# A hand-written instruction order for windowed attention with a gated convolution block: score folding, masking, biasing, convolution taps and reciprocals split into pieces of their own, and a new order of the period

## The chip, the cores and the metric

The kernel runs on one core of one Trainium2 chip. The metric is the device time of one execution in microseconds (us), measured over several executions; the profile is one further execution, recorded by the hardware profiler. A core has five instruction streams that matter here: TensorE (PE in the profile, with its weight loads shown apart as PEld), VectorE (DVE), ScalarE (ACT), GpSimd (POOL) and SyncE (SP, which here only issues DMAs). Each stream is executed in the order in which it was written; streams wait for each other on semaphores.

## The reference

Attention over 8 batches, 8 heads, 576 positions and head size 64, in a causal window of 128 with a linear distance bias, followed by a block that projects 512 to 1024 channels, applies a three-tap convolution along the sequence, gates with a sigmoid and projects back. All of it is in float32.

```python
scores = scale * np.matmul(q, k.transpose(0, 1, 3, 2))
bias = slopes[:, None, None] * (-np.abs(rel).astype(np.float32))[None, :, :]
mask = (rel >= 0) & (rel < window)
scores = np.where(mask, scores + bias[None], -1000000000.0)
scores = scores - np.max(scores, axis=-1, keepdims=True)
attn = np.exp(scores)
attn = attn / (np.sum(attn, axis=-1, keepdims=True) + 1e-09)
x = np.matmul(attn, v)
...
h = np.maximum(x @ w_in, 0.0)
for k in range(K):
    conv_out += conv_w[k][None, None, :] * hp[:, k:k + S, :]
gate = 1.0 / (1.0 + np.exp(-conv_out))
return (h * gate @ w_out)
```

## The kernel before

The 8 x 576 = 4608 tokens are cut into 36 tiles of 128, numbered t = 0 to 35, without regard to the batches' borders. Each tile's eight heads are worked in two groups of four, u = 0 and 1. Two tiles make a chunk of 256 columns for the convolution block; a chunk has four steps s, each over two blocks of 128 hidden channels, ff = 0 and 1. So a tile goes with two steps. The weights stay resident, each split into a high and a low part, and a product with full precision is three matmuls.

The order of all work is written out by hand. Three strings, OPENING, PERIOD and TAIL (lines 584 to 619), list pieces by short names; `emit` (line 570) calls the function behind each name, and under `tc.manual_schedule` every engine executes its instructions in just that order. OPENING holds tiles 0 to 5 and the splitting of the weights, PERIOD is emitted once for each of the 30 tiles 6 to 35, with the names' first number relative to the tile or to its first step, and TAIL finishes the last steps. In a name such as `T0.1` the first number is the tile (or step) and the second the group u (or the block ff); -1 is the tile or step before.

The pieces of a tile, with their engine, are:

- `S` (line 326, TensorE): the scores of one group, as many small matmuls, into two PSUM tiles `sc`, one for each half a = 0 and 1 of the group (two heads each). A query's window touches three blocks of 64 keys, of which two fill the 128 regular columns and the third 64 extra ones.
- `MA` (function `merge`, line 336, VectorE): for one half, a predicated copy that folds the extra columns into the regular ones (line 347); in tiles at a batch border (t mod 9 is 0, 4 or 5) one more predicated copy that writes a large negative value (line 355); then scale and bias, from PSUM into the SBUF tile `e` (line 358).
- `RM` (line 362, VectorE): the row extremum of the group's four heads. `X` (line 367, ScalarE): the exponentials with their sums, two heads to a piece.
- `N` (function `normal`, lines 378 and 379, VectorE): adds 1e-9 to the sums and takes the reciprocal. `M` (line 384, GpSimd): multiplies `e` by it.
- `T` (line 390, TensorE): four transposes of `e` into a PSUM tile `pa`. `RL` (line 395, ScalarE): copies that to SBUF as `rl`. `SEL` (lines 401 and 404, GpSimd): splits `rl` into the part for this tile's values and the part for the tile before.
- `AV` (line 420, TensorE): the product with the values for the tile before, group 0 first and then group 1. `XH` (line 431, ScalarE) and `XL` (line 435, VectorE) split the result into high and low part, and `XF` (lines 449 and 451, VectorE) copies one border column between neighbouring chunks. The first step of a chunk needs the border column of the tile behind it, so in every second period the period's first `UH` needs the `XF` of the same period.
- `QV` (line 244, VectorE): transposes the next tile's queries and keys. `LB`, `LV` (SyncE): loads.

The pieces of a step are:

- `UH` (line 464, TensorE): 12 matmuls into a PSUM tile `p`. `HH` (line 472, ScalarE): the rectifier. `Z` (line 478, ScalarE): the middle tap, into the PSUM tile `zp`, of which there is one buffer.
- `CV` (function `conv`, line 491, VectorE): the two outer taps, one after the other, both added in place into `zp`; where a batch border lies in the chunk, each tap is cut in two.
- `TH` (line 498, ScalarE): the tanh form of the gate. `GT` (line 502, VectorE): the gated product. `GH` (line 509, ScalarE) and `GL` (line 514, GpSimd): its high and low part.
- `D` (line 528, TensorE): 12 matmuls of the down projection. `OB` (line 538, ScalarE, and a store by SyncE): the result, every second period.

The PSUM tiles `sc`, `av`, `p` and `pa` share five buffers, and a new one takes a buffer that an earlier one has left.

Of the kernel before, what the change touches and what calls it, by code (L numbers as in the profile page):

```python
# [21 lines left out]
def tile_alibi_window_attention_conv_glu(  # L22
# [227 lines left out]
    raws, vraw, pts, sms, es, pas, rls, avs = {}, {}, {}, {}, {}, {}, {}, {}  # L250
# [82 lines left out]
        sms[t, u] = pss  # L333


    def merge(t, u, a):
# [10 lines left out]
        nc.vector.copy_predicated(  # L347
            out=s_all.rearrange("p g (c w) -> p g c w", w=QW),
            mask=m_same.rearrange("p (c w) -> p c w", w=QW).unsqueeze(1).to_broadcast([P, NG, NQ, QW]),
            data=extra,  # L350
        )
        negb = neg.unsqueeze(2).to_broadcast(shp)
        masks = [m for m, on in ((m_prev, first == 0), (m_half, first + P > S), (m_after, 0 < first < P)) if on]
        for mask in masks:
            nc.vector.copy_predicated(out=s_all, mask=mask.unsqueeze(1).to_broadcast(shp), data=negb)  # L355
# [2 lines left out]
        nc.vector.scalar_tensor_tensor(out=heads, in0=s_all, scalar=-0.125, in1=b, op0=ALU.mult, op1=ALU.add)  # L358

# [4 lines left out]
    def exps(t, u, heads=range(HU)):  # L364
        e, st, pss = sms[t, u]
        for j in heads:
            nc.scalar.activation(  # L367
                out=e[:, j, :],
                in_=e[:, j, :],
                func=AF.Exp,  # L370
                bias=st[:, 0, j : j + 1],
                scale=-1.0,
                accum_out=st[:, 1, j : j + 1],
            )

    def normal(t, u):
        e, st, pss = sms.pop((t, u))
        nc.vector.tensor_scalar(out=st[:, 2, :], in0=st[:, 1, :], scalar1=1e-9, scalar2=None, op0=ALU.add)
        nc.vector.reciprocal(out=st[:, 2, :], in_=st[:, 2, :])  # L379
        es[t, u] = e, st  # L380

# [97 lines left out]
            out=zps[s][:, ff, :], in_=hhs[s][:, ff, 1 : 1 + CW], func=AF.Copy, scale=cw[:, 1, f : f + 1]  # L479
        )  # L480

    def conv(s, ff):
# [4 lines left out]
        for kk, cuts in ((0, starts), (2, [x - 1 for x in starts])):
            a = 0
            for cut in [x for x in cuts if 0 <= x < CW] + [CW]:
                if cut > a:  # L490
                    nc.vector.scalar_tensor_tensor(  # L491
                        out=z[:, ff, a:cut], in0=hh[:, ff, a + kk : cut + kk], scalar=cw[:, kk, f : f + 1],
                        in1=z[:, ff, a:cut], op0=ALU.mult, op1=ALU.add,
                    )
                a = cut + 1

    def tanh(s):
        nc.scalar.activation(out=zps[s], in_=zps[s], func=AF.Tanh)  # L498
# [85 lines left out]
    OPENING = """
    LD0 F0 LD1 LV0 F1 F2 F3 F4 LD2 LV1 F5 Q0 CL0 QO0 S0.0 S0.1 RS0 Q1 MA0.0.0 MA0.1.0 MA0.1.1 MA0.0.1
    QO1 RM0.1 V0 F6 X0.1.1 S1.0 CL1 CL2 MA1.0.0 RM0.0 S1.1 X0.1.0 X0.0.0 MA1.0.1 X0.0.1 RS2 N0.1 M0.1 CL3
    RM1.0 N0.0 M0.0 H0 V2 T0.1 X1.0.0 RS1 T0.0 CL4 RL0.1 MA1.1.0 P0 V1 F7 F8 LD3 LV2 RS3 H2 X1.0.1 P2 W2
    RL0.0 MA1.1.1 RM1.1 SEL0.1 H1 SEL0.0 W0 P1 Q2 V3 F9 X1.1.1 AV0 W1 RS4 X1.1.0 N1.0 M1.0 N1.1 M1.1 CL7 V4 F10
    T1.0 H3 QO2 CL5 P3 T1.1 RL1.0 S2.0 RL1.1 MA2.0.0 S2.1 RS5 SEL1.1 MA2.0.1 MA2.1.0 CL6 RM2.0 SEL1.0
    MA2.1.1 X2.0.0 AV1 Q3 V5 F11 RS6 X2.0.1 H4 QO3 V6 F12 LD4 LV3 P4 W4 CL10 XH0 RM2.1 N2.0 M2.0 S3.0 XH1  # L590
    X2.1.1 X2.1.0 H6 H5 MA3.0.0 T2.0 CL8 N2.1 M2.1 MA3.0.1 RL2.0 T2.1 XL1 S3.1 W3 P5 P6 RM3.0 RL2.1 XL0 RS8
    CL9 MA3.1.0 SEL2.0 SEL2.1 XF1 RS7 W6 V7 F13 AV2 Q4 X3.0.0 W5 XF0 XH2 V8 F14 CL11 XL2 H7 QO4 X3.0.1
    P7 MA3.1.1 XF2 RS9 UH0.0 N3.0 M3.0 T3.0 W7 H8 HH0.0 CL12 Z0.0 RM3.1 UH1.0 X3.1.0 X3.1.1 HH1.0 V9 F15 P8
    UH1.1 CL14 RS11 CV0.0 UH0.1 RS10 RL3.0 H9 W8 N3.1 M3.1 HH0.1 T3.1 HH1.1 S4.0 V11 V10 F16 LD5 LV4 LD6 LV5
    LD7 Z0.1 RL3.1 CV0.1 H11 TH0 H10 MA4.0.0 P9 SEL3.0 RS12 GT0 GH0 SEL3.1 UH2.0 Z1.0 HH2.0 MA4.0.1
    CV1.0 RM4.0 P11 CL16 P10 AV3 LV6 W9 Z1.1 UH2.1 V12 W11 X4.0.1 X4.0.0 H12 CV1.1 P12 TH1 N4.0 M4.0 CL13 GT1
    XH3 GL0 W10 Z2.0 GH1 S4.1 XL3 CV2.0 CL15 UH3.0 HH2.1 Z2.1 MA4.1.0 HH3.0 RS13 CV2.1 D0 MA4.1.1 GL1
    RS15 TH2 W12 Q5 LD8 GT2 Q6 RS14 XF3 RM4.1 Z3.0 V13 UH3.1 QO5 V14 HH3.1 T4.0 CV3.0 H13 D1 QO6 X4.1.0
    Z3.1 X4.1.1 S5.0 V15 N4.1 M4.1 H14 MA5.0.0 RL4.0 P13 H15 P14 T4.1 SEL4.0 RL4.1 SEL4.1 CV3.1 MA5.0.1 W13
    GH2 W14 S5.1 P15 W15 GL2 MA5.1.0 AV4 LV7 TH3 XH4 RM5.0 GT3 X5.0.1 X5.0.0 XL4 D2 XF4 UH4.0 MA5.1.1  # L600
    GH3 RM5.1 RS16 HH4.0 V16 X5.1.0 N5.0 M5.0 Z4.0 H16 UH5.0 UH4.1 CV4.0 P16 X5.1.1 HH4.1 N5.1 M5.1 GL3 Z4.1 HH5.0
    T5.0 W16 CV4.1 UH5.1 RL5.0 T5.1 D3 TH4 SEL5.0 GT4 Z5.0 RL5.1 HH5.1 CV5.0 Z5.1 SEL5.1 GH4 CV5.1 TH5
    GT5 OB3 GL4
# [51 lines left out]
```

## Time and profile before

| | |
|---|---|
| median of 3 runs | 682.55 us (682.24 to 685.47) |
| the profiled execution | 681.73 us, span 680.0 us |
| mean granted TensorE clock | 0.987 |
| instructions | 15406 |
| busy share of the span | PE 91%, DVE 75%, ACT 62%, POOL 39% |

The span runs from the first to the last instruction. A timeline row gives start, duration, engine, line, operation, output <- inputs and a count of merged instructions; in brackets stands the idle time before it and what ended it. Rows of 30 periods repeat with small variations: border tiles carry three more kinds of mask, and some chunks cut their taps.

### The profile page before, as it was taken

To read this page: it belongs to the slowest core of one execution; us is meant where nothing else is said; L and a number is where in the kernel's file an instruction comes from. 1 tells how busy PE (TensorE), PEld (TensorE's weight loads), DVE (VectorE), ACT (ScalarE), POOL (GpSimd) and SP (SyncE) were. 2 spreads that over 40 slices of the span, in tenths; PEclk is the share of its full clock that TensorE was granted. 3 is DMA by queue.
4 is the path that set the end of the run, shared out by engine and by line. 5 is a ranking of instruction groups with operands and counts; after the bars stand their busy time and mean duration, and the time that the engine had idled before them with its cause. 6 is when DMAs were issued, how large, how long until landed. Compare 5 with 4: busy or idle time off the path is not lost.

```text
span 680.0 us, 15406 instructions
## 1 busy us (share of the span) xinstructions
PE 615.8 (91%) x5881; PEld 529.3 (78%) x5881; DVE 509.6 (75%) x1213; ACT 421.9 (62%) x1221; POOL 265.6 (39%) x307
## 2 busy tenths in 40 slices
...
PEclk9689999999999999999999999999999999999999
...
DMA packets 175534, 47.16 MB, mean 69 GB/s; under 512 B 168780, under 2 KB 168804, under 8 KB 175460
## 3 DMA queue, kind: packets, MB, share of 16 engines
...
## 4 chain that ended last, share of the span: by engine, by line
DVE 39%; PE 36%; ACT 11%; issue 8%; POOL 4%; DMA 1%; SPq 0%; POOLq 0%; DVEq 0%; ACTq 0%
DVE zp L491 15%; PE o L528 14%; PE p L464 9%; PE av L420 5%; ACT zp L478 5%; PE sc L326 4%; DVE e L358 4%; DVE sc L347 3%; DVE sc L355 3%; DVE st L362 3%; DVE z L502 3%; DVE qkT_all L244 2%; ACT zp L498 2%; POOL e L384 2%; PE pa L390 2%
## 5 line engine op out<-in xcount | busy, mean ns | idle before, releaser
L491 DVE SCALAR_TENSOR_TENSOR zp<-hh,cw,zp 128x256 f32<-128x256 f32 (+7 forms) x384 | 161.7, 421 | 90.4 <-ACT zp L478 81.7
L464 PEld LDWEIGHTS p<-x,wi 128*128 128x128 f32 x1728 | 212.0, 189 | 14.1 <-issue 9.1
L464 PE MATMUL p<-x,wi 128*128 128x258 f32 x1728 | 215.5, 283 | 7.3 <-DVE x L449 7.3
L528 PE MATMUL o<-wo,gh 128*128 128x512 f32 x576 | 187.0, 405 | 1.5 <-ACT gh L509 1.5
L384 POOL TENSOR_TENSOR e<-e,st 128x512 f32<-128x512 f32 x72 | 75.1, 1044 | 283.8 <-DVE st L379 229.0
L367 ACT ACTIVATE e<-e,st 128x128 f32<-128x128 f32 x288 | 112.0, 392 | 22.0 <-DVE st L362 22.0
L528 PEld LDWEIGHTS o<-wo,gh 128*128 128x128 f32 x576 | 102.8, 188 | 27.5 <-issue 4.8
L528 PE MATMUL o<-wo,gl 128*128 128x512 f32 x288 | 114.3, 397 | 0.6 <-POOL gl L514 0.6
L514 POOL TENSOR_TENSOR gl<-z,gh 128x512 fp32r<-128x512 f32 x72 | 92.3, 1282 | 42.9 <-ACT gh L509 41.9
L472 ACT ACTIVATE hh<-p 128x258 f32<-128x258 f32 x144 | 55.1, 383 | 84.0 <-PE p L464 84.0
L478 ACT ACTIVATE zp<-hh,cw 128x256 f32<-128x256 f32 x144 | 68.8, 478 | 48.3 <-DVE zp L491 43.2
L390 PE MATMUL pa<-ident_r,e 128*128 128x128 f32 x288 | 46.5, 285 | 41.2 <-POOL e L384 40.8
L502 DVE SCALAR_TENSOR_TENSOR z<-zp,hh 128x512 f32<-128x512 f32 x72 | 49.8, 691 | 43.5 <-ACT zp L498 43.5
L390 PEld LDWEIGHTS pa<-ident_r,e 128*128 128x128 f32 x288 | 32.4, 142 | 51.4 <-POOL e L384 50.7
L420 PE MATMUL av<-rl,rv 128*64 128x128 f32 x1088 | 68.9, 280 | 1.8 <-POOL rl L404 1.1
L420 PEld LDWEIGHTS av<-rl,rv 128*64 128x64 f32 x1088 | 60.2, 139 | 6.6 <-issue 1.8
L326 PEld LDWEIGHTS sc<-qkT_all 64*64 64x64 f32 x1792 | 52.6, 138 | 16.2 <-DVE zp L491 9.9
L528 PEld LDWEIGHTS o<-wo,gl 128*128 128x128 f32 x288 | 54.1, 188 | 14.0 <-POOL gl L514 1.1
L347 DVE COPY_PREDICATED sc<-m_same,sc 128x256 f32<-128x256 uint8 x144 | 60.5, 420 | 5.9 <-PE sc L326 5.8
L358 DVE SCALAR_TENSOR_TENSOR e<-sc,bias 128x256 f32<-128x256 f32 x144 | 61.1, 425 | 4.9
L326 PE MATMUL sc<-qkT_all 64*64 64x128 f32 (+2 forms) x1792 | 59.6, 273 | 1.8 <-DVE e L358 0.8
L401 POOL TENSOR_SCALAR_AFFINE_SELECT rl<-rl 128x512 f32<-128x512 f32 x64 | 41.2, 644 | 46.9 <-ACT rl L395 46.8
...
## 6 DMA issues: line engine op xcount, KB each, us to landing
...
```

The lines of the kernel that those rows point to most:

```text
L326: nc.tensor.matmul(strip(pss[a][qs, g, :], [to for to, _ in run]), qkT_all[rows, 0, u, g, base + c * QW : base + (c + 1) * QW], strip(qkT_ ...
L347: nc.vector.copy_predicated(out=s_all.rearrange("p g (c w) -> p g c w", w=QW), mask=m_same.rearrange("p (c w) -> p c w", w=QW).unsqueeze(1 ...
L358: nc.vector.scalar_tensor_tensor(out=heads, in0=s_all, scalar=-0.125, in1=b, op0=ALU.mult, op1=ALU.add)
L367: nc.scalar.activation(out=e[:, j, :], in_=e[:, j, :], func=AF.Exp, bias=st[:, 0, j : j + 1], scale=-1.0, accum_out=st[:, 1, j : j + 1],)
L384: nc.gpsimd.tensor_tensor(out=e, in0=e, in1=st[:, 2, :].unsqueeze(2).to_broadcast([P, HU, P]), op=ALU.mult)
L390: nc.tensor.transpose(ps[:, j, :], e[:, j, :], ident)
L420: nc.tensor.matmul(ps[g * D : (g + 1) * D, 2 * a + u], vraw[tt][:, a * HU + 2 * u + g], rl[:, side, 2 * g + a], start=n == 0, stop=n == le ...
L464: nc.tensor.matmul(ps[:, :XW], a[:, cc, f * P : (f + 1) * P], x[:, cc, :], start=n == 0, stop=n == last)
L478: nc.scalar.activation(out=zps[s][:, ff, :], in_=hhs[s][:, ff, 1 : 1 + CW], func=AF.Copy, scale=cw[:, 1, f : f + 1])
L491: nc.vector.scalar_tensor_tensor(out=z[:, ff, a:cut], in0=hh[:, ff, a + kk : cut + kk], scalar=cw[:, kk, f : f + 1], in1=z[:, ff, a:cut], ...
L514: nc.gpsimd.tensor_tensor(out=gl, in0=zgs.pop(s), in1=as32(gh), op=ALU.subtract)
L528: nc.tensor.matmul(oos[c][m], g[:, ff, ms], w[:, f, :], start=f == 0 and n == 0, stop=f == NFC - 1 and n == 2)
```

## The change

`merge` becomes three functions, `fold` (PU), `mask` (MK) and `biased` (BI), each for one half of a group. `normal` becomes `guard` (AD, the addition) and `invert` (RC, the reciprocal). `conv` now does one outer tap at a call, named by a third number 0 or 2. No instruction is added or removed by this.

In OPENING and TAIL the new names stand one behind the other where the old name stood. PERIOD is written anew:

```diff
     PERIOD = """
-    S0.0 MA0.0.0 S0.1 GH-1 AV-1 LV2 LB0 XH-1 MA0.0.1 RM0.0 MA0.1.0 XL-1 XF-1 D-2 OB-2 X0.0.0 X0.0.1 UH0.0 HH0.0
-    Z0.0 UH0.1 HH0.1 MA0.1.1 GL-1 UH1.0 RM0.1 QV1 X0.1.0 CV0.0 N0.0 M0.0 Z0.1 UH1.1 T0.0 X0.1.1 HH1.0
-    CV0.1 TH0 RL0.0 N0.1 M0.1 HH1.1 Q1 LD3 GT0 SEL0.0 Z1.0 QO1 CV1.0 T0.1 Z1.1 RL0.1 CV1.1 GH0 SEL0.1 TH1 GT1
-    GL0 D-1 OB-1
+    LD3 LB0 S0.0 S0.1 AV-1 PU0.0.1 PU0.0.0 MK0.0.1 MK0.0.0 D-2 XH-1 LV2 BI0.0.1 GH-1 XL-1 GL-1 BI0.0.0 XF-1
+    RM0.0 PU0.1.0 X0.0.1 OB-2 PU0.1.1 MK0.1.0 MK0.1.1 UH0.0 QV1 X0.0.0 UH0.1 BI0.1.1 HH0.0 AD0.0 BI0.1.0 Z0.0
+    CV0.0.0 UH1.0 HH0.1 RC0.0 RM0.1 M0.0 Z0.1 CV0.1.0 UH1.1 HH1.0 CV0.0.2 X0.1.0 CV0.1.2 X0.1.1 T0.0 Q1 D-1 TH0
+    AD0.1 RC0.1 RL0.0 M0.1 GT0 HH1.1 Z1.0 QO1 SEL0.0 Z1.1 CV1.0.0 GH0 CV1.0.2 T0.1 CV1.1.0 RL0.1 OB-1 CV1.1.2
+    SEL0.1 TH1 GT1 GL0
     """
```

The functions, cut to their core:

```diff
-    def merge(t, u, a):
+    def fold(t, u, a):
+        ps = scored(t, u, a)
...
-        for mask in masks:
-            nc.vector.copy_predicated(out=s_all, mask=mask.unsqueeze(1).to_broadcast(shp), data=negb)
+    def mask(t, u, a):
+        first = (t * P) % S
...
+        for m in masks:
+            nc.vector.copy_predicated(out=s_all, mask=m.unsqueeze(1).to_broadcast(shp), data=negb)
+
+    def biased(t, u, a):
...
-    def normal(t, u):
+    def guard(t, u):
+        e, st, pss = sms[t, u]
+        nc.vector.tensor_scalar(out=st[:, 2, :], in0=st[:, 1, :], scalar1=1e-9, scalar2=None, op0=ALU.add)
+
+    def invert(t, u):
         e, st, pss = sms.pop((t, u))
-        nc.vector.tensor_scalar(out=st[:, 2, :], in0=st[:, 1, :], scalar1=1e-9, scalar2=None, op0=ALU.add)
         nc.vector.reciprocal(out=st[:, 2, :], in_=st[:, 2, :])
...
-    def conv(s, ff):
+    def conv(s, ff, kk):
...
-        for kk, cuts in ((0, starts), (2, [x - 1 for x in starts])):
-            a = 0
```

On TensorE one piece moves, the second group's transposes `T0.1`. This is the end of tile 20's up projection before (`pa20_0` and `pa20_1` are the transposes of the two groups, `o8` is the down projection `D-1`):

```order
L390 MATMUL pa20_0_4552<-ident_r_81,e20_0_4411 128x128 x4
L390 MATMUL pa20_1_4578<-ident_r_81,e20_1_4456 128x128 x4
L528 MATMUL o8_0_4463<-wo0_123,gh33_4429 128x512
L528 MATMUL o8_0_4463<-wo1_124,gh33_4429 128x512
L528 MATMUL o8_0_4463<-wo0_123,gl33_4430 128x512
L528 MATMUL o8_1_4464<-wo0_123,gh33_4429 128x512
```

And this is the end of the same tile's period in the change, where the 12 matmuls of `o8` come first and the next tile's scores (`sc21`) follow `pa20_1`:

```order
L536 MATMUL o8_1_4447<-wo0_123,gh33_4465 128x512
L536 MATMUL o8_1_4447<-wo1_124,gh33_4465 128x512
L536 MATMUL o8_1_4447<-wo0_123,gl33_4466 128x512
L400 MATMUL pa20_1_4594<-ident_r_81,e20_1_4474 128x128 x4
L326 MATMUL sc21_0_0_4609<-qkT_all_127 64x128
L326 MATMUL sc21_0_1_4610<-qkT_all_127 64x128
```

The transposes of the second group have moved from ahead of 12 matmuls of `D-1` to behind them, and now stand straight ahead of the next tile's scores. All else on TensorE keeps its order.

On VectorE the beginning of the period changes. Before, from the last gated product of the tile before (`z33`) on (`sc20` are the scores, `e20` the biased scores, `x9` the low part `XL`, `x10` the border column `XF`):

```order
L502 SCALAR_TENSOR_TENSOR z33_4376<-zp33_4356,hh33_4341 128x512
L347 COPY_PREDICATED sc20_0_0_4397<-m_same_99,sc20_0_0_4397 128x2x128
L358 SCALAR_TENSOR_TENSOR e20_0_4411<-sc20_0_0_4397,bias_112 128x2x128
L347 COPY_PREDICATED sc20_0_1_4398<-m_same_99,sc20_0_1_4398 128x2x128
L358 SCALAR_TENSOR_TENSOR e20_0_4411<-sc20_0_1_4398,bias_112 128x2x128
L362 TENSOR_REDUCE st20_0_4412<-e20_0_4411 128x4
L347 COPY_PREDICATED sc20_1_0_4415<-m_same_99,sc20_1_0_4415 128x2x128
L358 SCALAR_TENSOR_TENSOR e20_1_4456<-sc20_1_0_4415,bias_112 128x2x128
L435 TENSOR_TENSOR x9_4044<-av19_4432,x9_4044 128x4x128
L451 CAST x10_4461<-x9_4044 128x8
```

In the change:

```order
L510 SCALAR_TENSOR_TENSOR z33_4394<-zp33_4366,hh33_4332 128x512
L346 COPY_PREDICATED sc20_0_1_4398<-m_same_99,sc20_0_1_4398 128x2x128
L346 COPY_PREDICATED sc20_0_0_4397<-m_same_99,sc20_0_0_4397 128x2x128
L365 SCALAR_TENSOR_TENSOR e20_0_4442<-sc20_0_1_4398,bias_112 128x2x128
L445 TENSOR_TENSOR x9_4053<-av19_4425,x9_4053 128x4x128
L365 SCALAR_TENSOR_TENSOR e20_0_4442<-sc20_0_0_4397,bias_112 128x2x128
L461 CAST x10_4471<-x9_4053 128x8
L369 TENSOR_REDUCE st20_0_4443<-e20_0_4442 128x4
L346 COPY_PREDICATED sc20_1_0_4411<-m_same_99,sc20_1_0_4411 128x2x128
L346 COPY_PREDICATED sc20_1_1_4412<-m_same_99,sc20_1_1_4412 128x2x128
```

The two halves' passes alternate, so that a pass rarely follows the one whose result it reads, and `XL` and `XF` have moved ahead of the first group's extremum. Further on, the four tap passes of the period's first step alternate between its two blocks, and `AD` and `RC` stand apart.

On ScalarE, `RL0.1` has moved behind `GH0` and stands ahead of `OB-1` and `TH1` at the end of the period; before, it stood ahead of `GH0` and `TH1`, with `OB-1` last. `GH-1` stands behind `XH-1` now. GpSimd's order is the same as before.

The five shared PSUM buffers are handed out by release, so their takers change too. In tile 20 the period's four `UH` take the buffers left by `BI0.0.1`, `XL`, `BI0.0.0` and `HH0.0`, and `T0.0` and `T0.1` those left by `BI0.1.1` and `BI0.1.0`. Before, the four `UH` and `T0.0` took those left by the first group's two `MA`, the second group's first `MA`, `XL` and the second group's second `MA`, and `T0.1` the one left by `HH0.0`.

More of the change, by code (lines that the diff above doesn't have):

```diff
@@ L333, in scores, with scored @@
         sms[t, u] = pss
-    def merge(t, u, a):
-        first = (t * P) % S
+    def scored(t, u, a):
         if len(sms[t, u]) == 2:
@@ L480, in middle @@
         )
-    def conv(s, ff):
+    def conv(s, ff, kk):
         c, f = s // NFP, 2 * (s % NFP) + ff
         hh, z = hhs[s], zps[s]
-        starts = [b * S - c * CW for b in range(1, B)]
-        starts = [x for x in starts if 0 <= x <= CW]
-        for kk, cuts in ((0, starts), (2, [x - 1 for x in starts])):
-            a = 0
[L489 to L495, printed above, removed]
+        starts = [b * S - c * CW - kk // 2 for b in range(1, B)]
+        a = 0
+        for cut in [x for x in starts if 0 <= x < CW] + [CW]:
+            if cut > a:
+                nc.vector.scalar_tensor_tensor(
+                    out=z[:, ff, a:cut], in0=hh[:, ff, a + kk : cut + kk], scalar=cw[:, kk, f : f + 1],
+                    in1=z[:, ff, a:cut], op0=ALU.mult, op1=ALU.add,
+                )
+            a = cut + 1
     def tanh(s):
@@ L584, in tile_alibi_window_attention_conv_glu @@
     OPENING = """
[L585 to L603, printed above, removed]
+    LD0 F0 LD1 LV0 F1 F2 F3 F4 LD2 LV1 F5 Q0 CL0 QO0 S0.0 S0.1 RS0 Q1 PU0.0.0 MK0.0.0 BI0.0.0 PU0.1.0 MK0.1.0
+    BI0.1.0 PU0.1.1 MK0.1.1 BI0.1.1 PU0.0.1 MK0.0.1 BI0.0.1 QO1 RM0.1 V0 F6 X0.1.1 S1.0 CL1 CL2 PU1.0.0 MK1.0.0
@@ new lines, in tile_alibi_window_attention_conv_glu @@
+    BI1.0.0 RM0.0 S1.1 X0.1.0 X0.0.0 PU1.0.1 MK1.0.1 BI1.0.1 X0.0.1 RS2 AD0.1 RC0.1 M0.1 CL3 RM1.0 AD0.0 RC0.0
+    M0.0 H0 V2 T0.1 X1.0.0 RS1 T0.0 CL4 RL0.1 PU1.1.0 MK1.1.0 BI1.1.0 P0 V1 F7 F8 LD3 LV2 RS3 H2 X1.0.1 P2 W2
+    RL0.0 PU1.1.1 MK1.1.1 BI1.1.1 RM1.1 SEL0.1 H1 SEL0.0 W0 P1 Q2 V3 F9 X1.1.1 AV0 W1 RS4 X1.1.0 AD1.0 RC1.0
+    M1.0 AD1.1 RC1.1 M1.1 CL7 V4 F10 T1.0 H3 QO2 CL5 P3 T1.1 RL1.0 S2.0 RL1.1 PU2.0.0 MK2.0.0 BI2.0.0 S2.1 RS5
+    SEL1.1 PU2.0.1 MK2.0.1 BI2.0.1 PU2.1.0 MK2.1.0 BI2.1.0 CL6 RM2.0 SEL1.0 PU2.1.1 MK2.1.1 BI2.1.1 X2.0.0 AV1
@@ new lines, in tile_alibi_window_attention_conv_glu @@
+    Q3 V5 F11 RS6 X2.0.1 H4 QO3 V6 F12 LD4 LV3 P4 W4 CL10 XH0 RM2.1 AD2.0 RC2.0 M2.0 S3.0 XH1 X2.1.1 X2.1.0 H6
+    H5 PU3.0.0 MK3.0.0 BI3.0.0 T2.0 CL8 AD2.1 RC2.1 M2.1 PU3.0.1 MK3.0.1 BI3.0.1 RL2.0 T2.1 XL1 S3.1 W3 P5 P6
+    RM3.0 RL2.1 XL0 RS8 CL9 PU3.1.0 MK3.1.0 BI3.1.0 SEL2.0 SEL2.1 XF1 RS7 W6 V7 F13 AV2 Q4 X3.0.0 W5 XF0 XH2 V8
+    F14 CL11 XL2 H7 QO4 X3.0.1 P7 PU3.1.1 MK3.1.1 BI3.1.1 XF2 RS9 UH0.0 AD3.0 RC3.0 M3.0 T3.0 W7 H8 HH0.0 CL12
+    Z0.0 RM3.1 UH1.0 X3.1.0 X3.1.1 HH1.0 V9 F15 P8 UH1.1 CL14 RS11 CV0.0.0 CV0.0.2 UH0.1 RS10 RL3.0 H9 W8 AD3.1
```

38 lines of the change are left out of this document (25 added, 13 removed).

## The prediction

> **What bounds the kernel now.** I read the page's shares first, then TensorE's waits over the 30 periods, then the timeline of one ordinary period, engine by engine. The page:
>
> ```profile
> PE 615.8 (91%) x5881; PEld 529.3 (78%) x5881; DVE 509.6 (75%) x1213; ACT 421.9 (62%) x1221; POOL 265.6 (39%) x307
> PEclk9689999999999999999999999999999999999999
> DVE 39%; PE 36%; ACT 11%; issue 8%; POOL 4%; DMA 1%; SPq 0%; POOLq 0%; DVEq 0%; ACTq 0%
> ```
>
> TensorE is busy for 91%, and after the opening its clock is not held back. The chain that ended last runs through VectorE more than through TensorE, so the share alone doesn't say which engine sets the period. TensorE's own waits between 130 and 640 us do:
>
> ```profile
> PE pa L390 <- POOL e L384: 30.8, 30, 1.4
> PE p L464 <- DVE x L449: 7.0, 6, 1.9
> ```
>
> There are two kinds. Once in each period the second group's transposes `T0.1` wait for GpSimd's product `M0.1`; and six times the first `UH` waits for the border column `XF`. One period of TensorE:
>
> ```profile
> 368.13 0.66 PE L390 MATMUL pa<-ident_r,e 128*128 128x128 f32 x4 [0.81 <-POOL e L384]
> 368.55 0.72 PE L528 MATMUL o<-wo,gh 128*128 128x512 f32 x2
> 371.52 1.57 PE L326 MATMUL sc<-qkT_all 64*64 64x128 f32 x64
> 373.02 1.97 PE L420 MATMUL av<-rl,rv 128*64 128x128 f32 x32
> 374.92 0.73 PE L528 MATMUL o<-wo,gh 128*128 128x512 f32 x2
> 377.82 5.90 PE L464 MATMUL p<-x,wi 128*128 128x258 f32 x48
> 383.56 0.60 PE L390 MATMUL pa<-ident_r,e 128*128 128x128 f32 x4
> 384.97 0.66 PE L390 MATMUL pa<-ident_r,e 128*128 128x128 f32 x4 [0.82 <-POOL e L384]
> ```
>
> Starts follow each other without a hole up to 383.56. Four transposes take 0.42 us of the stream (368.13 to 368.55), so TensorE's own work in the period is 383.56 - 368.13 + 0.42 = 15.85 us, and the period took 384.97 - 368.13 = 16.84. The 0.99 between them is the wait of 0.82 and 0.17 more, since a drained pipe shows its last matmul's tail as busy. Everything else on TensorE is full, so TensorE bounds the period, and these waits are what a new order can win.
>
> **The change part by part.** *T0.1 behind D-1.* It removes the wait if `M0.1` is done by then, and puts `RL0.1`, `SEL0.1` and the second half of the next `AV` close behind it. *XL and XF earlier on VectorE.* These take the six waits. *Passes of the halves alternating.* This shortens VectorE's way through a period; no term of the sum comes from it. All of this holds only if nothing is newly late, so I walk the new order through one ordinary period with durations from these rows:
>
> ```profile
> 356.21 0.42 DVE L358 SCALAR_TENSOR_TENSOR e<-sc,bias 128x256 f32<-128x256 f32 x1
> 356.55 0.42 DVE L347 COPY_PREDICATED sc<-m_same,sc 128x256 f32<-128x256 uint8 x1
> 357.00 0.42 DVE L358 SCALAR_TENSOR_TENSOR e<-sc,bias 128x256 f32<-128x256 f32 x1
> 357.46 0.69 DVE L362 TENSOR_REDUCE st<-e 128x4 f32<-128x512 f32 x1
> 358.06 0.42 DVE L347 COPY_PREDICATED sc<-m_same,sc 128x256 f32<-128x256 uint8 x1
> 358.86 0.68 DVE L435 TENSOR_TENSOR x<-av,x 128x512 fp32r<-128x512 f32 x1
> 361.17 1.30 DVE L244 STREAM_TRANSPOSE qkT_all<-arena 128x512 f32<-128x512 f32 x2
> 363.54 1.01 DVE L491 SCALAR_TENSOR_TENSOR zp<-hh,cw,zp 128x256 f32<-128x256 f32 x2 [1.07 <-ACT zp L478]
> 364.46 0.16 DVE L378 TENSOR_SCALAR st<-st 128x4 f32<-128x4 f32 x1
> 364.66 0.18 DVE L379 RECIPROCAL st<-st 128x4 f32<-128x4 f32 x1
> 372.00 0.69 DVE L502 SCALAR_TENSOR_TENSOR z<-zp,hh 128x512 f32<-128x512 f32 x1 [0.72 <-ACT zp L498]
> ```
>
> On VectorE a pass that reads the result of the one before starts 0.45 behind it (356.55 to 357.00), one that doesn't 0.34 (356.21 to 356.55), that is before the other's 0.42 are over. [...]
>
> ```profile
> 354.95 1.08 ACT L538 COPY ob<-o 128x512 f32<-128x512 f32 x2
> 358.19 0.59 ACT L431 CAST x<-av 128x512 fp32r<-128x512 f32 x1 [1.65 <-PE av L420]
> 364.33 0.39 ACT L367 ACTIVATE e<-e,st 128x128 f32<-128x128 f32 x1
> 366.27 0.37 ACT L472 ACTIVATE hh<-p 128x258 f32<-128x258 f32 x1
> 366.64 0.58 ACT L498 ACTIVATE zp<-zp 128x512 f32<-128x512 f32 x1
> 367.37 0.59 ACT L395 COPY rl<-pa 128x512 f32<-128x512 f32 x1
> 367.85 0.39 ACT L472 ACTIVATE hh<-p 128x258 f32<-128x258 f32 x1
> 368.13 0.48 ACT L478 ACTIVATE zp<-hh,cw 128x256 f32<-128x256 f32 x1
> 370.65 0.61 ACT L509 CAST gh<-z 128x512 fp32r<-128x512 f32 x1
> 367.04 1.04 POOL L384 TENSOR_TENSOR e<-e,st 128x512 f32<-128x512 f32 x1 [1.02 <-DVE st L379]
> 368.03 0.64 POOL L401 TENSOR_SCALAR_AFFINE_SELECT rl<-rl 128x512 f32<-128x512 f32 x1
> 368.74 0.64 POOL L404 TENSOR_SCALAR_AFFINE_SELECT rl<-rl 128x512 f32<-128x512 f32 x1
> 372.12 1.28 POOL L514 TENSOR_TENSOR gl<-z,gh 128x512 fp32r<-128x512 f32 x1
> ```
>
> Zero is the first matmul of `S0.0`. If TensorE never waits, `AV-1` starts at 1.50, `D-2` at 3.40, `UH0.0` at 6.30, each further `UH` 1.44 later (5.74 for four), `T0.0` at 12.04, `D-1` at 12.46, `T0.1` at 15.43, the next `S0.0` at 15.85.
>
> The tile before's `T0.1` started at -0.42 and ended at 0.24. `RL0.1` runs from 0.28 to 0.87, `SEL0.1` from 0.94 (0.07 later, as 367.96 to 368.03) to 0.94 + 0.71 + 0.64 = 2.29. The second half of `AV-1` is due at 1.50 + 0.95 = 2.45: on time by 0.1. `GL0` follows on GpSimd to 3.53, and `D-2` needs it with its third matmul, at about 3.40 + 0.48 (two of the twelve in 2.9).
>
> `TH1` follows `RL0.1` at 0.76, `GT1` at 1.40, the two `PU` at 2.00 and 2.34, the first `BI` at 2.68; in every second period `OB-1` puts 1.08 ahead of that. `XL` then waits for `XH`: `AV` ends at 3.47, `XH` takes 3.51 to 4.10, `XL` 4.18 to 4.86. VectorE stands idle here for about a microsecond. The second `BI` ends at 5.20, `XF` at 5.33, 0.97 ahead of `UH0.0`, so the wait for `XF` goes; `RM0.0` ends at 5.93. Four exponentials (0.39 each) end at 7.6; `HH0.0` is due at 7.94. On VectorE `PU`, `PU`, `QV`, `BI`, `AD`, `BI` end at 8.7, when `Z0.0` is done as well. `CV0.0.0` starts at 8.74, `RC0.0` at 9.14, `RM0.1` ends at 9.93, and the other three taps end at 11.46. `M0.0` is done at 10.4 (due 12.04). `X0.1` ends at 12.65, `RC0.1` at 13.05, `M0.1` at 14.15: 1.28 ahead of `T0.1`. `TH0` ends at 13.24, `GT0` at 13.99, the two `Z` of the second step at 14.93, `GH0` at 15.46, so ScalarE is free for `RL0.1` at 16.13; the four taps end at 16.5, and `TH1` starts at 16.61, which is 0.76 in the next period. The walk closes on itself, and no TensorE piece waits.
>
> Border tiles put four more passes on VectorE, 0.49 each:
>
> ```profile
> L355 DVE COPY_PREDICATED_SCALAR sc<-m_prev,neg 128x256 f32 x12 | 5.8, 487 | 0.4
> 163.88 1.10 PE L326 MATMUL sc<-qkT_all 64*64 64x64 f32 x32
> ```
>
> At a step of about 0.4 the first two fall into the idle microsecond ahead of `XL`, and the other two come out of slack: 0.7 behind an `OB` they leave `M0.0` some 0.2 ahead of `T0.0`. Cut taps add about 0.3 a tap, hidden in the wait for `X0.1` and in that ahead of `XL`.
>
> The sum: the 30 waits give 30.8 and 30 x 0.17 = 5.1, the six others 7.0: 42.9 us. Back go: three times the next tile's `S` takes 1.0, not 1.5 (the second row above), so the second half of `AV` is due at 1.95 and waits 0.4 until 2.29 + 0.05, 1.2 in all; and behind the last tile there is no `S` at all, where `AV`'s first half covers 0.95 of the same 2.34, 1.4. Net 42.9 - 2.6 = 40.3. The profiled execution took 681.73, so 641.4; the median of the runs is 0.8 above it. I say **642**. The loads and stores on SyncE pass each other (`LB0` now ahead of `LV2`), which costs nothing: the loads are for tiles well ahead. OPENING and TAIL keep their order, at nothing.
>
> Its own range: if nothing at all goes back, 681.73 - 42.9 = 638.8, and a microsecond below for the tails; above, the 0.1 us ahead of `AV` may be 0.2 short in each period, 6 us, 648.
>
> **The rivals.** *A wait behind the moved transposes.* `RL0.1` and `SEL0.1` had 3.0 of `D-1` and 1.5 of `S` to hide in, and have `S` and half of `AV` now. For it: only 0.1 is spare. Against it: that half-`AV` cover, and ScalarE free 0.6 early. If it comes 0.5 late in each period, 15 us go back: 642 + 15 = 657.
>
> *The ScalarE-VectorE chain takes the bound.* From `T0.1` round to `M0.1` is 14.57 long by the walk (-0.42 to 14.15) against a period of 15.85, over some twenty handovers. If each cost 0.1 more than I take, 2.0 eat the 1.28, and the period is 0.7 longer: 21 us back, 663. For it: VectorE's 39% of the chain, and `XL`, which now blocks VectorE until `XH` is done. Against it: the rows above have the handovers in them.
>
> *Slower than before: M0.1 late.* Before, a wait of `T0.1` was followed by `D-1`, which covered `RL0.1` and `SEL0.1`; now it stands bare. The change decides against itself once `M0.1` slips past 15.43 by more than the 42.9 / 30 = 1.43 that a period lost before, so by 1.28 + 1.43 = 2.7 us on the walk. At 3.2 late, 0.5 more is lost in each period: 682 + 15 = 697. For it: `RM0.1` stands behind more on VectorE now. Against it: nothing on the walk slips by over a microsecond.
>
> **How the numbers follow.** The walk as it stands 0.70; the first rival 0.15; the second 0.08; all given back, within 0.5% (3.4 us, about what a measurement can tell from no change) 0.04; the third 0.03. Faster is the first three, 0.93. The range takes in the forecast's own 637 to 648 and the first rival's 657: 637 to 658, and leaves out the rest.
>
> **What would show it.** Right: in TensorE's waits the row of `pa` for GpSimd and that of `p` for the border column are gone or a few us; ordinary periods of about 15.85; VectorE idle ahead of `XL`, for `XH`. The first rival would show as waits of `av` for GpSimd's `rl`, or of `o` for `gl`; the second and third as `pa` waiting for `e` at the period's end, short and long. It is wrong if TensorE has no such waits and the periods stay at 16.8, or if a granted clock below 1.00 stretches TensorE's own work.

## The result and the profile after

The change takes 643.69 us (median of 4 runs, 640.61 to 644.22) where the kernel before takes 682.91 on the same chip: a ratio of 0.941, 95% interval 0.9371 to 0.9448. The forecast was 642. The profiled execution took 644.22 us, its span 642.5.

The shares of the page and the chain that ended last, after the change:

```profile
PE 609.0 (95%) x5881; PEld 531.0 (83%) x5881; DVE 494.0 (77%) x1213; ACT 422.5 (66%) x1221; POOL 265.8 (41%) x307
PE 67%; DVE 18%; issue 7%; ACT 4%; POOL 2%; DMA 1%; POOLq 0%; SPq 0%; DVEq 0%; ACTq 0%
```

The chain has moved to TensorE, from 36% to 67%. TensorE's own waits in the 30 periods (130 to 605 us) are now:

```profile
PE p L474 <- DVE x L459: 3.0, 4, 0.8
PE av L430 <- POOL rl L414: 1.1, 1, 1.1
```

All 30 waits of the transposes are gone; four of the six waits of the first `UH` for the border column remain, shorter; and the one wait of `av` is the one behind the last tile. An ordinary period of TensorE:

```profile
336.78 0.60 PE L400 MATMUL pa<-ident_r,e 128*128 128x128 f32 x4
337.30 1.57 PE L326 MATMUL sc<-qkT_all 64*64 64x192 f32 x48
...
352.60 0.60 PE L400 MATMUL pa<-ident_r,e 128*128 128x128 f32 x4
```

From `T0.1` to `T0.1` it is 352.60 - 336.78 = 15.82 us, with no hole, where 15.85 was worked out. VectorE and GpSimd beside it (the score matmuls start at 337.30):

```profile
339.57 0.69 DVE L510 SCALAR_TENSOR_TENSOR z<-zp,hh 128x512 f32<-128x512 f32 x1 [0.95 <-ACT zp L506]
340.18 0.75 DVE L346 COPY_PREDICATED sc<-m_same,sc 128x256 f32<-128x256 uint8 x2
341.44 0.69 DVE L445 TENSOR_TENSOR x<-av,x 128x512 fp32r<-128x512 f32 x1 [0.18 <-ACT x L441]
342.05 0.41 DVE L365 SCALAR_TENSOR_TENSOR e<-sc,bias 128x256 f32<-128x256 f32 x1
342.38 0.94 DVE L461 CAST x<-x 128x8 fp32r<-128x8 f32 x1
343.23 0.67 DVE L369 TENSOR_REDUCE st<-e 128x4 f32<-128x512 f32 x1
342.00 1.29 POOL L522 TENSOR_TENSOR gl<-z,gh 128x512 fp32r<-128x512 f32 x1 [1.35 <-ACT gh L517]
350.59 1.04 POOL L394 TENSOR_TENSOR e<-e,st 128x512 f32<-128x512 f32 x1 [2.43 <-ACT zp L506]
```

`XL` starts 4.14 behind the scores (4.18 in the walk) and waits for `XH` as expected: 0.18 here, behind an `OB-1`. `XF` takes 0.94, not 0.17, so `RM0.0` ends at 6.60 instead of 5.93. `M0.1` is done at 14.33 (14.15), 0.97 ahead of `T0.1` at 15.30.

Cut at the first scores of tile 6 and at the first matmul behind the last tile, the two executions compare so (before, then after):

```profile
0.00:112.00 112.00, 91.72 (x777) 0.92 0.51 137
112.00:631.80 519.80, 481.66 (x4833) 1.00 0.28 58
631.80:680.00 48.20, 42.40 (x273) 0.99 0.09 34
```

```profile
0.00:114.00 114.00, 90.43 (x777) 0.91 0.50 135
114.00:591.50 477.50, 474.41 (x4833) 1.00 0.31 63
591.50:642.50 51.00, 44.14 (x273) 0.96 0.08 32
```

The columns are the stretch, its length, TensorE's busy time with the count of matmuls, its granted clock, and the DMA's share and rate. The 30 periods are 42.3 us shorter (forecast 42.9 - 1.2). The end is 2.8 longer: 1.3 is the wait behind the last tile (forecast 1.4), the rest goes with a lower granted clock, and so does the opening's 2.0, whose order is unchanged.

### The profile page after: what moved, and what is told of

It reads as the page before. It is cut to its first block, busy times and chain, and to the rows that moved or that the text cites. A ratio compares the mean times of both kernels' runs of the same rounds, so it can differ in the third digit from the quotient of the medians.

```text
span 642.5 us, 15352 instructions
## 1 busy us (share of the span) xinstructions
PE 609.0 (95%) x5881; PEld 531.0 (83%) x5881; DVE 494.0 (77%) x1213; ACT 422.5 (66%) x1221; POOL 265.8 (41%) x307
## 4 chain that ended last, share of the span: by engine, by line
PE 67%; DVE 18%; issue 7%; ACT 4%; POOL 2%; DMA 1%; POOLq 0%; SPq 0%; DVEq 0%; ACTq 0%
PE p L474 24%; PE o L536 23%; PE av L430 7%; PE sc L326 7%; DVE zp L499 5%; PE pa L400 4%; DVE sc L346 2%; DVE e L365 2%; POOL gl L522 2%; DVE arena L188 1%; DVE arena L191 1%; PE pw L207 1%; DVE z L510 1%; DVE st L369 1%; ACT zp L506 1%
## 5 line engine op out<-in xcount | busy, mean ns | idle before, releaser
L506 ACT ACTIVATE zp<-zp 128x512 f32<-128x512 f32 x72 | 42.2, 586 | 35.9 <-DVE zp L499 33.8
L430 PEld LDWEIGHTS av<-rl,rv 128*64 128x64 f32 x1088 | 58.6, 137 | 8.7 <-POOL rl L414 3.6
L346 DVE COPY_PREDICATED sc<-m_same,sc 128x256 f32<-128x256 uint8 x144 | 55.0, 419 | 6.6 <-PE sc L326 6.6
L365 DVE SCALAR_TENSOR_TENSOR e<-sc,bias 128x256 f32<-128x256 f32 x144 | 58.8, 410 | 0.9
L374 ACT ACTIVATION_READ_ACCUMULATOR e<-e,st 128x1 f32 x288 | 54.4, 189 | 0.0
```

The lines of the kernel that those rows point to most:

```text
L346: nc.vector.copy_predicated(out=ps[:, :, :P].rearrange("p g (c w) -> p g c w", w=QW), mask=m_same.rearrange("p (c w) -> p c w", w=QW).unsq ...
L374: nc.scalar.activation(out=e[:, j, :], in_=e[:, j, :], func=AF.Exp, bias=st[:, 0, j : j + 1], scale=-1.0, accum_out=st[:, 1, j : j + 1],)
L430: nc.tensor.matmul(ps[g * D : (g + 1) * D, 2 * a + u], vraw[tt][:, a * HU + 2 * u + g], rl[:, side, 2 * g + a], start=n == 0, stop=n == le ...
```

## The experiments

The forecast's reason (theory A) was that the moved transposes and the earlier `XL` and `XF` carry the gain, and the alternating passes nothing. The rival (B) was that the alternating passes carry it. Seven kernels were made for these two, and then five for what they left open. Times are medians; the kernel before took 683.2 to 683.5 beside them. The rows of TensorE's waits in this section are those between 125 and 600 us, which leaves out the last period or two of the longer kernels.

One table for all, the length of a period from its first score matmul to the next one's, in us. Tile 20 is ordinary, 26 has its taps cut, 22 is a border tile, 13 a border tile in an odd place behind a chunk with cut taps:

| kernel | median | tile 20 | 26 | 22 | 13 |
|---|---|---|---|---|---|
| before | 682.91 | 16.84 | 17.44 | 17.33 | 18.49 |
| the change | 643.69 | 15.83 | 15.83 | 15.83 | 16.79 |
| T0.1 moved alone | 681.09 | 15.83 | 17.25 | 17.47 | 19.18 |
| T0.1 moved back | 692.97 | 17.80 | 17.79 | 17.82 | 17.83 |
| passes in series | 663.70 | 15.82 | 16.65 | 17.09 | 18.22 |
| XL late | 665.72 | 15.82 | 15.83 | 15.81 | 20.62 |
| XL first | 660.62 | 15.83 | 16.65 | 17.07 | 17.98 |
| scores alone in series | 655.78 | 15.82 | 15.91 | 16.42 | 18.34 |
| taps alone together | 649.34 | 15.83 | 16.12 | 16.18 | 17.06 |
| in series, M0.0 early | 668.85 | 15.83 | 17.13 | 17.01 | 18.37 |
| combined | 646.21 | 15.82 | 15.82 | 15.81 | 17.12 |

**T0.1 moved alone** (the kernel before, PERIOD):

```diff
-    ... GT0 SEL0.0 Z1.0 QO1 CV1.0 T0.1 Z1.1 RL0.1 CV1.1 GH0 SEL0.1 TH1 GT1
-    GL0 D-1 OB-1
+    ... GT0 SEL0.0 Z1.0 QO1 CV1.0 D-1 T0.1 Z1.1 RL0.1 CV1.1 GH0 SEL0.1 TH1 GT1
+    GL0 OB-1
```

> The kernel before with one piece moved: D-1 ahead of T0.1 in the period; nothing else. Theory A (the moved transposes carry the gain): the 30 waits of the transposes go, 30.8 + 5.1 us; about 2.6 comes back behind them; XL stays behind two passes more than in the change and now starts from a later GT1, so the waits of UH for the border column grow from 7 to about 12. Time 650 to 658, most likely 655. Theory B (the alternating passes, which shorten VectorE's way, carry it): the wait moves elsewhere, 670 or more.

Measured: 681.09 us, ratio 0.9961 (0.9943 to 0.9978). The forecast's reason fails here. TensorE's waits:

```profile
PE p L464 <- DVE x L449: 14.2, 7, 2.6
PE pa L390 <- POOL e L384: 10.2, 11, 1.6
PE av L420 <- POOL rl L404: 2.4, 10, 0.3
```

In the ordinary tiles 20 and 24 the move does all that was forecast (15.83 and 15.82); other ordinary tiles give a part of it back (16.16 in tile 21) or more (17.61 in tile 17, 16.93 before). In cut and border tiles new waits take it back, and the waits for the border column double. In tile 22 VectorE's first fold started 1.08 behind the scores before and starts 2.41 behind them here, and `M0.0` ends at 13.59, where `T0.0` is due at 12.05; before, it ended at 12.26. Of these 1.34 us, 1.04 are there already at the last `Z` of the tile before (from 1.78 to 0.74 ahead of the scores). The other 0.30 goes with ScalarE's own wait for the moved transposes at `RL0.1`, behind which `TH1` and so the gated product stand:

```profile
387.49 0.59 ACT L395 COPY rl<-pa 128x512 f32<-128x512 f32 x1 [0.37 <-PE pa L390]
```

**T0.1 moved back** (the change, PERIOD):

```diff
-    ... CV0.1.2 X0.1.1 T0.0 Q1 D-1 TH0
+    ... CV0.1.2 X0.1.1 T0.0 Q1 TH0
...
-    ... CV1.0.2 T0.1 CV1.1.0 RL0.1 ...
+    ... CV1.0.2 T0.1 D-1 CV1.1.0 RL0.1 ...
```

> The change with one piece moved back: T0.1 ahead of D-1 again; all else of the new order, alternating passes included, stays. Theory A: M0.1 is done at about 14.2 in the walk and T0.1 would be due at 12.5, so TensorE waits 1.7 to 1.9 in each of 30 periods: 643.7 + 52 = about 695, slower than the kernel before. Theory B: below 665, since VectorE's way stays short.

Measured: 692.97 us, ratio 1.0144 (1.0109 to 1.0178), 1.4% slower than before, as theory A said and B did not.

```profile
PE pa L400 <- POOL e L394: 45.4, 27, 1.8
```

So B falls as well: the new order without the moved transposes loses 10 us, the moved transposes without the new order win 2, and both together win 39.

**Passes in series** (the change, PERIOD):

```diff
-    ... PU0.0.1 PU0.0.0 MK0.0.1 MK0.0.0 D-2 XH-1 LV2 BI0.0.1 GH-1 XL-1 GL-1 BI0.0.0 XF-1
+    ... PU0.0.1 MK0.0.1 BI0.0.1 PU0.0.0 MK0.0.0 BI0.0.0 D-2 XH-1 LV2 GH-1 XL-1 GL-1 XF-1
-    RM0.0 PU0.1.0 X0.0.1 OB-2 PU0.1.1 MK0.1.0 MK0.1.1 UH0.0 QV1 X0.0.0 UH0.1 BI0.1.1 HH0.0 AD0.0 BI0.1.0 Z0.0
+    RM0.0 PU0.1.0 MK0.1.0 BI0.1.0 X0.0.1 OB-2 PU0.1.1 MK0.1.1 BI0.1.1 UH0.0 QV1 X0.0.0 UH0.1 HH0.0 Z0.0
-    CV0.0.0 UH1.0 HH0.1 RC0.0 RM0.1 M0.0 Z0.1 CV0.1.0 UH1.1 HH1.0 CV0.0.2 X0.1.0 CV0.1.2 ...
+    CV0.0.0 CV0.0.2 UH1.0 HH0.1 AD0.0 RC0.0 RM0.1 M0.0 Z0.1 CV0.1.0 UH1.1 HH1.0 CV0.1.2 X0.1.0 ...
```

> The change with the passes of the halves one behind the other again: fold, mask and bias of one half, then of the other; both taps of the first step's first block together; AD and RC together. T0.1 stays behind D-1, XL and XF stay ahead of the first extremum. Theory A: VectorE has slack ahead of XL and ahead of AD0.1, so no TensorE wait comes of it: 642 to 646. Theory B: about 0.1 us more for each of some eight passes on VectorE's way, 0.9 a period, 27 in all: 670.

Measured: 663.70 us, ratio 0.9705 (0.9683 to 0.9728): 20 us above the change. The alternating passes, to which the forecast gave no term, are worth half the gain, nearly all of it in cut and border tiles (the eight ordinary periods lose 0.7 us together). The second group's six score passes in border tile 22, in the change and then in series:

```profile
375.47 0.74 DVE L346 COPY_PREDICATED sc<-m_same,sc 128x256 f32<-128x256 uint8 x2
376.13 0.86 DVE L359 COPY_PREDICATED_SCALAR sc<-m_half,neg 128x256 f32 x2
376.91 1.29 DVE L244 STREAM_TRANSPOSE qkT_all<-arena 128x512 f32<-128x512 f32 x2
378.13 0.38 DVE L365 SCALAR_TENSOR_TENSOR e<-sc,bias 128x256 f32<-128x256 f32 x1
378.44 0.15 DVE L385 TENSOR_SCALAR st<-st 128x4 f32<-128x4 f32 x1
378.50 0.41 DVE L365 SCALAR_TENSOR_TENSOR e<-sc,bias 128x256 f32<-128x256 f32 x1
378.83 0.47 DVE L499 SCALAR_TENSOR_TENSOR zp<-hh,cw,zp 128x255 f32<-128x255 f32 x1
```

```profile
385.96 0.42 DVE L346 COPY_PREDICATED sc<-m_same,sc 128x256 f32<-128x256 uint8 x1
386.41 0.49 DVE L359 COPY_PREDICATED_SCALAR sc<-m_half,neg 128x256 f32 x1
386.93 0.42 DVE L365 SCALAR_TENSOR_TENSOR e<-sc,bias 128x256 f32<-128x256 f32 x1
387.28 0.42 DVE L346 COPY_PREDICATED sc<-m_same,sc 128x256 f32<-128x256 uint8 x1
387.73 0.49 DVE L359 COPY_PREDICATED_SCALAR sc<-m_half,neg 128x256 f32 x1
388.25 0.42 DVE L365 SCALAR_TENSOR_TENSOR e<-sc,bias 128x256 f32<-128x256 f32 x1
388.59 1.29 DVE L244 STREAM_TRANSPOSE qkT_all<-arena 128x512 f32<-128x512 f32 x2
```

In series the six take 388.59 - 385.96 = 2.63; alternating, 1.44 for the four ahead of the transposes and 0.31 + 0.33 for the two biases, 2.08. With the taps and `AD` moved too, `M0.0` in this tile ends 13.20 behind the scores in series and 11.62 in the change, and `T0.0` is due at 12.05 to 12.06. So the change had 0.43 to spare there and the series kernel waits:

```profile
392.31 0.66 PE L400 MATMUL pa<-ident_r,e 128*128 128x128 f32 x4 [1.04 <-POOL e L394]
```

**XL first** (the change with `XL` and `XF` ahead of masks and biases):

```diff
-    ... MK0.0.1 MK0.0.0 D-2 XH-1 LV2 BI0.0.1 GH-1 XL-1 GL-1 BI0.0.0 XF-1
+    ... D-2 XH-1 XL-1 XF-1 MK0.0.1 MK0.0.0 LV2 BI0.0.1 GH-1 GL-1 BI0.0.0
```

> The change with XL and XF ahead of the masks and the biases of the first group. Theory A: the four waits of UH for the border column that the change still has (3.0 us, in odd border tiles behind a chunk with cut taps) go; the first extremum ends 0.5 later, inside ScalarE's slack ahead of HH0.0: about 640.7 where the change has 643.7, and no row of UH waiting for the border column. Rival: the later extremum pushes X0.0, HH0.0 and M0.1 past their due times, and waits of the transposes appear: 645 or more.

Measured: 660.62 us, ratio 0.9659 (0.9637 to 0.968). The rival was right. The waits for the border column fall to 1.4 us, but 15 waits of the transposes, 11.3 us in all, appear:

```profile
PE pa L400 <- POOL e L394: 11.3, 15, 1.1
PE p L474 <- DVE x L459: 1.4, 6, 0.2
```

They are `T0.0`, not `T0.1`: VectorE waits for `XH` ahead of the masks now, and in tile 22 `M0.0` ends at 13.18.

**XL late** (the change with `XL` and `XF` behind the second group's masks):

```diff
-    ... BI0.0.1 GH-1 XL-1 GL-1 BI0.0.0 XF-1
+    ... BI0.0.1 GH-1 GL-1 BI0.0.0
-    ... MK0.1.0 MK0.1.1 UH0.0 ...
+    ... MK0.1.0 MK0.1.1 XL-1 XF-1 UH0.0 ...
```

> The change with XL and XF moved back behind the second group's folds and masks, where they stand about as late as before. Theory A: in ordinary tiles XF still ends ahead of UH0.0 (5.8 against 6.3), in odd border tiles it ends 1 to 2 us late: the waits of UH for the border column go from 3.0 us to 6 to 9 us, and the time is 646 to 650. Rival (the early XL gains nothing and only blocks VectorE until XH is done): same as or below the change, 643.7.

Measured: 665.72 us, ratio 0.9744 (0.9718 to 0.9769). The direction was right, the size too small: seven waits for the border column make 16.4 us, up to 3.2 each. In the odd border tiles 27 and 31 the period is 21.7, but 20.6 in tiles 9 and 13, with the same waits; the granted clock was halved for 6.8 us in each of the former and for 3.4 us in each of the latter (last section).

**M0.1 longer by one pass, and by three** (the change, in `weigh`; the factor 1.0 leaves the result as it is):

```diff
+        for _ in range(1 if u == 1 and t >= FIRST else 0):
+            nc.gpsimd.tensor_scalar(out=e, in0=e, scalar1=1.0, scalar2=None, op0=ALU.mult)
```

> The change with one more GpSimd pass (times 1.0, in place, about 0.6 us) behind M0.1 in each period; the result is the same. Theory A: M0.1 is done 1.28 us ahead of T0.1, so 0.6 costs nothing: 643 to 646. Rival (the chain from T0.1 round to M0.1 is as long as the period): 0.6 x 30 = 18 more, 662.

> As the one before with three such passes, about 1.9 us. Theory A: 1.28 of it is free, 0.6 and 0.17 of drained pipe are not, in 30 periods: 643.7 + 23 = 667, with 30 waits of the transposes for GpSimd of about 0.6. Rival (no slack): 643.7 + 56 = 700.

Measured: 660.52 us (0.9663, 0.9637 to 0.9689) and 807.08 us (1.1807, 1.1767 to 1.1848). Both expectations rested on 0.6 us for a pass. It took 1.49:

```profile
358.69 1.04 POOL L394 TENSOR_TENSOR e<-e,st 128x512 f32<-128x512 f32 x1 [2.43 <-ACT zp L508]
359.82 1.49 POOL L396 TENSOR_SCALAR e<-e 128x512 f32<-128x512 f32 x1
```

From the end of `M0.1` alone (359.73) to the end of the pass (361.31) that is 1.58; 0.97 of it was free, and the other 0.61 shows in most periods, with 0.11 more (16.55 for 15.83 in tile 20). So the slack of `M0.1` is about a microsecond in all tiles. Only where TensorE waited for the border column before (tiles 9, 13, 27 and 31) is the period hardly longer, 0.1 at most: the later scores take the place of that wait. With three passes the waits are 3.65 to 3.71 in all periods but the first two, and the clock goes as well (last section).

The first seven left this theory (C): the shorter period lays VectorE's line later against TensorE, and the piece that is late first is `M0.0` ahead of `T0.0`. **Scores alone in series** and **taps alone together** are the two halves of the series edit above:

> Theory C, after the first seven runs: with T0.1 moved, TensorE no longer waits for M0.1 and its period is a microsecond shorter, so VectorE's line lies a microsecond later against it, and the next piece that is due is M0.0 ahead of T0.0 (due 12.05 behind the first score matmul; in the change it is done at 10.9 in ordinary, 11.2 in cut, 11.6 in border tiles). Alternating passes buy that. This kernel is the change with only fold, mask and bias in series (the taps, AD and RC as in the change). Theory C: border tiles lose 0.9 on the way to M0.0 and wait 0.4 to 0.7 for it, ordinary ones don't wait: 646 to 653. Theory A (alternation is worth nothing, the loss in the series kernel came from its other edits): 643.7.

> The other part alone: the change with both taps of the first step's first block together, and AD and RC together behind them; the score passes alternate. Theory C: M0.0 comes 0.6 to 0.9 later, which cut and border tiles lack by 0.1 to 0.5: 645 to 651. Theory A: 643.7. Both parts together gave 663.7; since each has its own slack first, theory C has them add up to less than the 20 us.

Measured: 655.78 us (0.9589, 0.9561 to 0.9619) and 649.34 us (0.9486, 0.945 to 0.9521). The sum of both losses, 12 and 6, is 18 of the 20. The scores cost more than expected, and by another way than theory C's: 7.8 us of waits for the border column against 2.0 for the transposes.

```profile
PE p L474 <- DVE x L459: 7.8, 7, 1.6
PE pa L400 <- POOL e L394: 2.0, 4, 0.6
```

**In series, M0.0 early** (the series kernel with `AD0.0 RC0.0 M0.0` ahead of `QV1`):

```diff
-    ... UH0.0 QV1 X0.0.0 UH0.1 HH0.0 Z0.0
-    CV0.0.0 CV0.0.2 UH1.0 HH0.1 AD0.0 RC0.0 RM0.1 M0.0 Z0.1 ...
+    ... UH0.0 X0.0.0 UH0.1 AD0.0 RC0.0 M0.0 QV1 HH0.0 Z0.0
+    CV0.0.0 CV0.0.2 UH1.0 HH0.1 RM0.1 Z0.1 ...
```

> The series kernel (663.7) with AD, RC and M of the first group moved ahead of QV and the taps; no pass alternates. Theory C: M0.0 is done at 10.5 to 11.5 in all tiles, the waits of the transposes go from 12.0 us to under 4, and the time is 648 to 654; what stays are the waits of UH for the border column (5.5 us). Rival (the alternating itself is what counts): 660 or more.

Measured: 668.85 us, ratio 0.9779 (0.9751 to 0.9807). Theory C in this narrow form falls. `M0.0` is early now (11.45 in tile 22, due 12.05), but `RM0.1` ends at 12.95 there (11.01 in the change), `M0.1` at 16.37, and `T0.1` is due at 15.3:

```profile
PE pa L400 <- POOL e L394: 9.6, 14, 1.1
PE p L474 <- DVE x L459: 8.0, 7, 1.6
```

It is VectorE's whole line, from the last gated product to `RM0.1`, that is too long in cut and border tiles without the alternating. Moving one piece ahead passes the lateness to the next.

**GH first** (the change with `GH-1` ahead of `XH-1`):

```diff
-    ... D-2 XH-1 LV2 BI0.0.1 GH-1 XL-1 ...
+    ... D-2 GH-1 XH-1 LV2 BI0.0.1 XL-1 ...
```

> The change with GH-1 ahead of XH-1 on ScalarE, so that GpSimd's GL-1 has run before XF comes. In the change XF, a cast of 8 elements, takes 0.94 us where it falls into GL-1 on GpSimd and 0.17 where it doesn't (before: 0.17 always). If GpSimd's pass blocks the cast, XF takes about 0.2 in all ordinary tiles here and the first extremum ends about 0.65 earlier in tiles without a store ahead (5.95 for 6.60); the time stays within 641 to 646, since that lies in slack. Rival (the cast is slow for its own reasons, such as its place behind XL): 0.94 stays.

Measured: 643.42 us, ratio 0.9408 (0.938 to 0.9436), the same as the change within the noise. `XF` on VectorE between 130 and 590 us, in the change and then here:

```profile
L459 DVE CAST x<-x 128x8 fp32r<-128x8 f32 x15 | 8.9, 592 | 0.0
L461 DVE CAST x<-x 128x8 fp32r<-128x8 f32 x14 | 5.4, 388 | 0.0
```

```profile
L459 DVE CAST x<-x 128x8 fp32r<-128x8 f32 x15 | 2.5, 164 | 0.0
L461 DVE CAST x<-x 128x8 fp32r<-128x8 f32 x14 | 2.3, 164 | 0.0
```

`RM0.0` ends at 5.88 in tile 21, not 6.60, and the time doesn't care, as expected.

**Combined** (`GH` first; `XL XF` between masks and biases; `RC0.0 M0.0` ahead of the first tap):

```diff
-    ... D-2 XH-1 LV2 BI0.0.1 GH-1 XL-1 GL-1 BI0.0.0 XF-1
+    ... D-2 GH-1 XH-1 LV2 XL-1 XF-1 BI0.0.1 GL-1 BI0.0.0
-    CV0.0.0 UH1.0 HH0.1 RC0.0 RM0.1 M0.0 Z0.1 ...
+    RC0.0 M0.0 CV0.0.0 UH1.0 HH0.1 RM0.1 Z0.1 ...
```

> What the runs point to: the change with GH-1 ahead of XH-1 (XF no longer blocked by GL-1), XL and XF straight behind the masks and ahead of both biases, and RC and M of the first group ahead of the first tap. Border tiles in odd places: XF about 0.65 earlier, so the waits of UH for the border column go from 3 to 4 us to about 1; M0.0 0.4 earlier, so T0.0 doesn't take the wait over. Ordinary periods stay at 15.83. Expected 640 to 642, against 643.7 for the change. Rival (lateness only passes on to the next piece due, as in the last series kernel): 643.5 or more.

Measured: 646.21 us, ratio 0.9455 (0.9436 to 0.9473). The rival was right again: the four waits for the border column shrink from 0.7 or 0.8 to 0.4 each, but two more of 0.26 appear, six tiles' `AV` now waits 0.26 for `SEL0.1`, and some cut and border tiles lose 0.1 to 0.2. No version here beats the change.

## Why the prediction was right, and where it was not

*The size.* The 30 periods gave 42.3 where 41.7 was forecast, the wait behind the last tile cost 1.3 for 1.4, and the forecast of 642 is missed by 1.7. What it lacked is outside its terms: the opening and the end lost about 3.5 to a lower granted clock. That the periods came so close is in part luck. By the rows above TensorE's idle time in them fell by 35.05 (38.14 to 3.09), where 36.6 was forecast (30.8 + 7.0 - 1.2), and its busy time, which holds the tails of drained pipes, by 7.25, where 5.1 was: the waits that stayed and the tails that were taken too short nearly cancel.

*The step that failed* is "Passes of the halves alternating ... no term of the sum comes from it". In series the kernel takes 20 us more. The walk itself used the shorter steps of alternating passes (0.34 from `PU` to `PU`), so its total held what this sentence puts at nothing. It was right that an ordinary tile doesn't need them: in tile 20 every order with `T0.1` behind `D-1` and nothing lengthened runs at 15.82 or 15.83. But it was made through an ordinary tile, and cut and border tiles were settled in three sentences, "come out of slack". There the slack was 0.43 at `M0.0` only because the passes alternate.

*What the forecast took as separate terms is one.* It gave the moved transposes a term of 35.9 us. By themselves they gave 2. Before, TensorE's wait for `M0.1` was also the time in which VectorE and ScalarE caught up; without it, VectorE's first pass of a tile lies 1.3 us later against TensorE (1.08 to 2.41 in tile 22, of which 0.3 is ScalarE's wait at `RL0.1`), and what had been on time or nearly so (`M0.0`, `XF`) is late. The forecast had this only as its second rival, at 0.08, with the handovers as the point in dispute; the runs show it decided by the heaviest tiles. The new places of `RL0.1`, `OB-1` and `GH-1` on ScalarE came with the change too; only that of `GH-1` was tried apart, so what the other two are worth stays open.

*The early XL.* It was given 7.0 and the waits were to go; 3.0 stay, in tiles 9, 13, 27 and 31. Each is a border tile in an odd place behind a chunk with cut taps, so both of the things that the forecast had hidden in the same idle microsecond ahead of `XL` fall together. Putting `XL` back costs 22 us, far more than 7, for the same reason as above.

*The slack of M0.1* was 0.97, not 1.28: `M0.1` ended 0.18 later than walked, and `T0.1` came 0.13 sooner. The blocked `XF` (below) is not the reason, since `M0.1` ends at 14.33 with `GH` first as well. *Behind shorter scores* a loss of 1.2 was forecast. The rows of waits show none, but about 0.7 is there: in tiles 9, 18 and 27 the second half of `AV` starts 2.15 behind the scores, where it started at 1.96 in tile 18 before, and tile 18 with its shorter scores takes 15.60, about 0.24 more than these leave of 15.83. The wait is hidden under the tail of the first half, which shows as busy. *The third rival* (slower, by `M0.1` late ahead of a bare `T0.1`) needed 2.7 us; the extra passes show that it is real: past the slack, each period pays.

*What alternating does on VectorE* stands in the rows: the same six passes take 2.08 us and not 2.63. In tile 22 a 128x256 pass starts 0.46 behind the one whose result it reads (in series, 2.88 to 3.34 behind the scores) and 0.33 behind one that it doesn't depend on (in the change, 2.88 to 3.21). The Trainium skill (VectorE: DVE Perf Modes, The DRAIN you can't avoid) says that the next operation does not start until the pipe is empty, and that one which is not held back starts earlier. The independent passes here agree with the second half: they start before the 0.42 us of the one ahead are over.
